# One core, attention and a feed-forward layer in one kernel: the first batch's feed-forward reordered from interleaved halves to all of the first product and then the second

## The chip, the cores and the metric

The kernel runs on one core of one Trainium2 chip. The metric is the device time of one execution in microseconds. Below, PE is the matmul engine (TensorE), PEld its weight load, DVE is VectorE, ACT is ScalarE, POOL is GpSimd, and SP issues every DMA of this kernel from one queue, in program order. Each engine works off its own queue in order.

## The reference, cut to what matters

```python
batch, n_heads, seq, head_dim = (4, 8, 768, 64)          # attention
block, window = (32, 16)
k_sum = k.reshape(B, H, nb, block, D).max(axis=3)
v_sum = v.reshape(B, H, nb, block, D).mean(axis=3)
mask_l = np.abs(pos[:, None] - pos[None, :]) < window
scores_s = scale * np.einsum('bhsd,bhnd->bhsn', q, k_sum) + np.log(block)
scores_all = np.concatenate([np.where(mask_l, scores_l, -1e9), scores_s], axis=-1)
...
x = attn_out.transpose(0, 2, 1, 3).reshape(B, S, H * D)  # (4, 768, 512)
h = x.transpose(0, 2, 1) @ U @ V                          # U (768, 32), V (32, 768)
u = x + h.transpose(0, 2, 1)
ch = np.maximum(u @ w_ch1, 0.0) @ w_ch2                   # 512 -> 2048 -> 512
return (u + ch).astype(np.float32)
```

Every query sees 31 keys around it and 24 block summaries (largest key, mean value of 32 positions). `U`, `V`, `w_ch1` and `w_ch2` are float64.

## The kernel before, in words

The four batches go through the same stages: attention by heads, the low-rank mix that gives `u`, the first product with `w_ch1` (the up product, `NF` = 16 tiles of hidden channels), ReLU, the second product with `w_ch2` (the down product), and the sum with `u`. While PE works on one batch's up and down products, the attention of the next batch is spread over that time in small steps; heads are numbered `h` = 0 to 7. All engine queues are written out by hand: an instruction stands where the Python program emits it.

Matmuls in full precision are made of three in a faster format: a matrix is split in a high part (an ACT cast) and a low part (a subtraction on DVE or POOL), and high·high, high·low and low·high are added up. A weight tile arrives as float64 words (512 KB), ACT scales the upper words (L148), DVE puts the two words together in two operations (L160, L161) into a buffer of the tag `val`, ACT casts the high part (L176) and DVE or POOL subtracts for the low part (L177, `split`). The float32 weights and sums of them (`sum_weights`) also go to DRAM for the later batches.

The opening (the word list `START`) does batch 0's attention. Then comes batch 0's own loop: for every `f` of 16 and both halves `hf` of the tokens, `up` runs 12 matmuls of 384 columns for tile `f` (L1066), `up_out` applies the ReLU and splits, and `down_rows` runs 9 matmuls of 512 columns (L1088) for the half before. The outputs of batch 0 come out with tokens in rows and are turned back by 24 PE transposes (`finish_rows`, L1109) in the up phase of batch 1. The weights of `w_ch1` and `w_ch2` arrive side by side, each through a ring of five places. In the same loop the attention of batch 1 runs by steps of its own (`one_bank_steps`), with `scores` (L348: six score tiles a head, zero-padded queries, full array).

Batches 1 and 2 have another form: `up_phase` computes the up product with seven instead of eight block products (L1352) and copies the results to SBUF; then `down_phase` runs with channels in rows: for each `f`, 12 matmuls of 512 columns and 12 of 256 columns (L1450), after `gate_high` (ACT) and `gate_low` (DVE) have made the ReLU and its low part of 768 columns. The attention of batches 2 and 3 runs in the steps of `later_step`, with `scores_by_subtiles` (L371: 24 small matmuls a head). Batch 3 uses seven products in both phases. The splits of stored weights for these batches are made by `prepare` (ACT L1016, POOL or DVE L1012).

`add_vsum` sums 32 values a block for the summaries on POOL (L258 to L272); `drip` hands out one such operation at a time. `operands` makes the operands of the next batch's seven products from `u`: for batch 1 it calls `mix_u` (three PE transposes, L733, and one matmul, L741), for later batches `add_rows`.

Of the kernel before, what the change touches and what calls it, by code (L numbers as in the profile page):

```python
# [36 lines left out]
RING = 5  # L37
# [58 lines left out]
def body(ctx: ExitStack, tc, q0, q1, k, v, vn, uv, w1, w2, mask, ident, rep, out):  # L96
# [36 lines left out]
    qd0 = [t[:, j * NH : (j + 1) * NH] for j in range(3)] + [weight_place(1, 2)[:, :NH]]  # L133
# [102 lines left out]
    def load_vsum(st, g, i):  # L236
# [4 lines left out]
        if st.b == 1 or st.b == 2 and g == 0:  # L241
            spare = hidden_place(2 + i)
# [96 lines left out]
    def scores(st, h, a):  # L339
        if h not in st.neg:  # L340
            st.neg[h] = small.tile([P, NU], F32, name="neg", bufs=4)
        qt, kt = st.qt[h].rearrange("p u q -> p (u q)"), st.kt[h]
        ps = bank("ps_s")
        for i in range(3):
            u = 3 * a + i
            j = ORDER.index(u)
            k0 = (j // 2) * KP + (j % 2) * KC
            nc.tensor.matmul(  # L348
                ps[:, i * KC : (i + 1) * KC],
                qt[:, 64 + j * P : 64 + j * P + P],  # L350
                kt[:, k0 : k0 + KC],
                start=True,
                stop=True,
            )
# [1443 lines left out]
```

## Time and profile before

| | us |
|---|---|
| runs shown | 630.95, 627.56, 630.90; median 630.9 |
| the profiled execution, whole | 628.56 |
| its span, first to last instruction | 626.8 |
| opening, to the first matmul of batch 0's up product | 50.5 |
| batch 0's loop | 50.5 to 211.3 |
| batch 1's up and down phases | 211.3 to 278.2, 278.2 to 369 |
| PE busy | 608.7 |
| PEld, DVE, ACT, POOL busy | 554.9, 417.0, 364.4, 298.6 |

The profiled execution is 2.3 us below the median of the runs; they spread over 3.4 us. PE is the bound: it is busy for 97% of the span, at a mean granted clock of 0.997, and most of what it is not busy lies in the opening. A busy PE is not PE at its peak, since matmuls overlap: the time of a stage is read from the starts of successive instructions, not from their lengths.

### The profile page before, as it was taken

How to read it: one execution, taken by the hardware profiler on the slowest of the kernel's cores; microseconds unless marked ns; L12 is line 12 of the kernel's file. 1: busy time of each engine (PE TensorE's matmuls, PEld its weight loads, DVE VectorE, ACT ScalarE, POOL GpSimd, SP SyncE). 2: the span in 40 equal slices, each digit the busy share in tenths (PEclk: the TensorE clock that was granted, in tenths of full speed). 3: DMA queues.
4: the chain of work that ended last, by engine and by line, in shares of the span. 5: the costliest groups of instructions: out<-in, count | busy, mean ns of one | idle time of the engine just before them, and what ended most of it. 6: DMA issues, size and time to landing. Idle time of an engine off the chain costs nothing.

```text
span 626.8 us, 14616 instructions
## 1 busy us (share of the span) xinstructions
PE 608.7 (97%) x5384; PEld 554.9 (89%) x5384; DVE 417.0 (67%) x1141; ACT 364.4 (58%) x828; POOL 298.6 (48%) x361
## 2 busy tenths in 40 slices
PE   4989999999999999999999999999999999999997
PEld 3779988889888999998888889998888899999997
DVE  4868867665678696477548964566546754449992
ACT  4856666656555657665444456674644456669550
POOL 2621635523246875787556966774222256630000
PEclk9989999999999999999999999999999999999999
DMA  8898499997879169888995577889997563375551
GB/s 225 230 386 269 138 314 295 289 325 256 274 204 312 53 219 298 236 260 257 271 285 175 179 258 233 250 260 274 287 280 223 160 226 120 117 223 174 159 193 51
DMA packets 94215, 144.76 MB, mean 231 GB/s; under 512 B 8896, under 2 KB 64576, under 8 KB 94144
## 3 DMA queue, kind: packets, MB, share of 16 engines
q1 hardware_dynamic: 94144, 143.82, 74.5%
q8 instruction: 43, 0.70, 0.5%
q14 instruction: 28, 0.23, 0.1%
HBM read 102.89 MB, written 40.89 MB: 229 GB/s over the span
## 4 chain that ended last, share of the span: by engine, by line
PE 90%; DMA 3%; DVE 2%; SPq 2%; issue 1%; ACT 1%; POOL 1%; ACTq 0%; POOLq 0%
PE ps_h L1352 26%; PE acc L1450 22%; PE ps_h L1066 10%; PE acc L1088 10%; PE acc L1562 9%; PE ps_x L504 3%; PE ps_s L371 2%; PE ps_s L348 2%; SPq L212 1%; DMA place<-in_v 1%; PE ps_m L699 1%; PE ps_u L733 1%; DMA whole<-up 1%; DMA place<-in_k 1%; DVE val L161 1%
## 5 line engine op out<-in xcount | busy, mean ns | idle before, releaser
L1012 POOL TENSOR_TENSOR parts<-whole,parts 128x512 fp32r<-128x512 f32 (+1 forms) x128 | 159.0, 1250 | 135.6 <-ACT parts L1016 121.0
L1352 PE MATMUL ps_h<-op,parts 128*128 128x384 f32 x1008 | 181.9, 337 | 1.0 <-ACT place L1398 0.9
L1352 PEld LDWEIGHTS ps_h<-op,parts 128*128 128x128 f32 x1008 | 174.2, 188 | 3.7 <-ACT place L1398 1.2
L1450 PE MATMUL acc<-gh,parts 128*128 128x256 f32 (+1 forms) x512 | 135.3, 342 | 0.0
L1450 PEld LDWEIGHTS acc<-gh,parts 128*128 128x128 f32 x512 | 88.3, 189 | 12.9 <-issue 1.7
L1016 ACT CAST parts<-whole 128x512 fp32r<-128x512 f32 (+1 forms) x144 | 83.5, 585 | 10.5 <-DMA whole<-sums 4.3
L1450 PE MATMUL acc<-gl,parts 128*128 128x512 f32 (+1 forms) x256 | 86.6, 338 | 0.0
L177 POOL TENSOR_TENSOR place<-val,place 128x512 fp32r<-128x512 f32 x29 | 38.5, 1348 | 87.5 <-ACT place L176 74.5
L406 ACT ACTIVATE e<-e,neg 128x120 f32<-128x120 f32 x144 | 46.5, 386 | 54.0 <-DVE neg L396 53.9
L1066 PE MATMUL ps_h<-place 128*128 128x384 f32 x384 | 73.5, 340 | 0.0
L1066 PEld LDWEIGHTS ps_h<-place 128*128 128x128 f32 x384 | 67.0, 188 | 1.8 <-DVE val L161 0.2
L1088 PE MATMUL acc<-place,gh 128*128 128x512 f32 x192 | 66.4, 401 | 0.0
L1450 PEld LDWEIGHTS acc<-gl,parts 128*128 128x128 f32 x256 | 48.6, 190 | 3.9
L1425 DVE SCALAR_TENSOR_TENSOR gl<-place,gh 128x768 fp32r<-128x768 f32 x32 | 33.8, 1056 | 20.7 <-ACT gh L1421 20.6
L396 DVE CUSTOM_DVE_ANT_0 e<-ps_s,mask_sb 128x120 f32<-128x120 f32 x144 | 32.7, 277 | 17.7 <-PE ps_s L371 9.7
L1562 PE MATMUL acc<-place,parts 128*128 128x384 f32 x246 | 43.6, 334 | 0.0
L1562 PEld LDWEIGHTS acc<-place,parts 128*128 128x128 f32 x246 | 42.7, 188 | 0.0
L1088 PEld LDWEIGHTS acc<-place,gh 128*128 128x128 f32 x192 | 36.1, 188 | 7.3
L1421 ACT ACTIVATE gh<-place 128x768 fp32r<-128x768 f32 x32 | 27.0, 844 | 22.1 <-PE acc L1450 22.0
L1078 ACT ACTIVATE gh<-ps_h 128x384 fp32r<-128x384 f32 x32 | 15.7, 491 | 40.5 <-PE ps_h L1066 40.4
L1079 DVE SCALAR_TENSOR_TENSOR gl<-ps_h,gh 128x384 fp32r<-128x384 f32 x32 | 17.8, 555 | 30.5 <-ACT gh L1078 30.5
L1088 PE MATMUL acc<-place,gl 128*128 128x512 f32 x96 | 37.7, 393 | 0.0
(166 smaller groups left out, 960.1 us busy)
## 6 DMA issues: line engine op xcount, KB each, us to landing
place<-in_w SPq DMA_DIRECT2D x32, 512.0 KB, 6.8
whole<-up SPq DMA_DIRECT2D x24, 512.0 KB, 4.3
there<-squares SPq DMA_DIRECT2D x24, 384.0 KB, 5.0
at<-there SPq DMA_DIRECT2D x96, 96.0 KB, 4.2
whole<-up SPq DMA_DIRECT2D x24, 384.0 KB, 3.6
whole<-down SPq DMA_DIRECT2D x16, 512.0 KB, 4.9
vt<-in_v SPq DMA_DIRECT2D x48, 146.2 KB, 4.3
kt<-in_k SPq DMA_DIRECT2D x24, 288.0 KB, 5.7
```

The lines of the kernel that those rows point to most:

```text
L177: engine.tensor_tensor(lo, val, f32(hi), ALU.subtract)
L396: nc.vector.tensor_tensor_reduce(out=e[:, u, :], in0=ps[:, i * KC : (i + 1) * KC], in1=mask_sb[:, m, :], scale=-SCALE, scalar=BIG, op0=ALU ...
L406: nc.scalar.activation(e[:, u, :], e[:, u, :], AF.Exp, bias=st.neg[h][:, u : u + 1], scale=-1.0,)
L1012: engine.tensor_tensor(lo, whole, f32(hi), ALU.subtract)
L1016: nc.scalar.copy(hi, whole)
L1066: nc.tensor.matmul(ps[:, :NH], w_split[0, f][:, c % 2, part_w, c // 2], ut[:, c, :], start=(n == 0), stop=(n == 3 * NC - 1),)
L1088: nc.tensor.matmul(acc[t], gt[:, sl], w_split[1, f][:, part_w], start=(first and j == 0), stop=(last and j == 2),)
L1352: nc.tensor.matmul(ps, a[:, sa, i], b[:, sb, i], start=(first and n == 0), stop=(n == 5), skip_group_check=not first,)
L1421: nc.scalar.activation(gh, h, AF.Relu)
L1425: nc.vector.scalar_tensor_tensor(gl, h, 0.0, f32(gh), ALU.max, ALU.subtract)
L1450: nc.tensor.matmul(place, w[:, part_w, c * P : (c + 1) * P], gt[:, q0:q1], start=(f == 0 and i == 0 and j == 0), stop=(f == NF - 1 and j = ...
L1562: nc.tensor.matmul(ps, w[:, part_w, off : off + P], g[part_g], start=((name, i) not in begun and j == 0), stop=(p == NF // 2 - 1 and j == ...
```

## The change: what it does

Batch 0's up product is now done for all 16 tiles first. Each result is copied to SBUF by ACT (`hidden_place`), in the form that `down_phase` expects, and then `down_phase` does batch 0's down product with channels in rows, as for batches 1 and 2. Up comes in quarters: for every tile, two token halves with two halves of the 12 matmuls each. `u` of batch 0 is put together again as `x` by POOL (`keep_rows`, eight operations of 384 columns), since `down_phase` adds `x` at the end. `finish_rows`, `leave_rows`, `up_out`, `down_rows`, `scores` and `one_bank_steps` are gone.

The 32 weight tiles go one after the other, `w_ch1` first, through one ring of eight places; step `s` of `first_weights` loads tile `s+7`, scales `s+3`, puts together `s+2` and splits `s+1`. All low parts are made by POOL now; before, the first three were made by DVE. Batch 1's attention runs in `later_step`, with `scores_by_subtiles`; thirteen of its 32 steps lie in the up phase and the others in the down phase; its spreading of key maxima goes from ACT to POOL. For batch 1, `operands` still calls `mix_u` first, and the call with `k == 4`, which is now made for batch 1 too, does as well. In the opening seven weight tiles are loaded instead of ten, the two parts of `V`'s spreading (`Q`) stand together, the mix of the first channels stands earlier, and the first up tile for both token halves is inside the opening (`U`).

```diff
-RING = 5
+RING = 8
 START = """
...
-    T13 Q1 E15 N0 M1 Mo1 C11 N3 Bp5 I0 Bd6 T8 la1 Dd5 lr Z0 Io0 C10 Dp4 T15 lb0 Y0.0 T9 Y0.1 Bp4 Dp7
...
-    N7 Jo0 I2 Qo0 lb2 Io2 Y1.0 G0.0 Qo1 J2 G1.0 Y1.1 lb4 G0.1 G1.1 Go0.0 Jo2 G0.2 G0.3 W0 Go0.1
-    Go1.1 G1.3 Go0.2 Go0.3 Go1.3 G1.2 Go1.0 Go1.2 W1 lb3 U0.0 la2 Z2
+    T13 Q1 Q0 E15 N0 Qo1 Qo0 M1 Mo1 C11 N3 Bp5 I0 Bd6 T8 lw2 Dd5 Z0 Io0 C10 Dp4 T15 lw3 Y0.0 T9
...
+    V8 V12 C15 N4 V13 V15 V14 N6 G1.0 lw5 N7 Go0.0 Go0.1 I2 Io2 U0.0.0 G1.1 Go1.0 Go1.1 lw6 J2 Jo2
+    U0.1.0 G0.2 G0.3 Go0.2 Go0.3 G1.2 G1.3 Go1.2 Go1.3 U0.0.1 U0.1.1 W1 Z2
...
+        by = nc.gpsimd.tensor_copy if st.b == 1 else nc.scalar.copy if h == 0 else nc.vector.tensor_copy
+        spread_maxima(st, h, by)
...
-            split(hi, lo, val, nc.vector if k < 2 else nc.gpsimd)
+        split(hi, lo, val, nc.gpsimd)
...
+    def up(st, hf, f, half):
+
         uh, ul = st.u[hf]
+        if half == 0:
+            begun_up[hf, f] = bank("ps_h")
+        ps = begun_up[hf, f]
+        for c in (2 * half, 2 * half + 1):
+            for j, (part_w, ut) in enumerate(((0, uh), (0, ul), (1, uh))):
                 nc.tensor.matmul(
                     ps[:, :NH],
+                    w_split[f][:, c % 2, part_w, c // 2],
                     ut[:, c, :],
...
+        if half == 1:
+            p, k = divmod(f, 2)
+            if p not in st.h:
+                st.h[p] = hidden_place(p).rearrange("p (f q) -> p f q", f=2)
+            nc.scalar.copy(st.h[p][:, k, hf * NH : (hf + 1) * NH], begun_up.pop((hf, f))[:, :NH])
+
+    def keep_rows(st, hf, c):
+
         uh, ul = st.u[hf]
+        nc.gpsimd.tensor_tensor(
+            channel_rows(st, c)[:, 3 * hf : 3 * hf + 3],
+            *(f32(t)[:, c].rearrange("p (u q) -> p u q", q=P) for t in (uh, ul)),
+            ALU.add,
+        )
+
+    def first_up_phase(st, done):
+
+        for f, hf, half in itertools.product(range(NF), range(2), range(2)):
+            if (hf, f, half) not in done:
+                up(st, hf, f, half)
+            yield
...
+    def first_weights(s, q, n):
+
+
+        f = s % NF
+
+        def turn():
+            if s + 2 < 2 * NF:
+                if s + 2 not in turning:
+                    turning[s + 2] = turn_weight(s + 2)
+                run(turning[s + 2], 1 if q == 1 else None)
+
+        if q == 0:
+            if s + RING - 1 < 2 * NF:
+                load_weight(s + RING - 1)
+            if 0 < s and s + 1 < 2 * NF:
+                split_weight(s + 1)
+            if s < NF and f % 2 == 0:
+                sum_weights(f // 2, 0)
...
+        if q == 3 and s + 3 < 2 * NF:
+            scale_weight(s + 3)
...
+    UP0 = 4 * NF - 2
+    later_start(sts[1], -6)
+    later_start(sts[1], -5)
+    for b in range(B):
...
+        steps = spread(mine, 4 if b else 8, up_last)
+        if b == 0:
+            phase = first_up_phase(cur, done)
+            for n, j in enumerate((-4, -3, -2, -1)):
+                steps.setdefault(n + 1, []).append((later_start, ahead, j))
+            for n, (hf, c) in enumerate(itertools.product(range(2), range(NC))):
+                steps.setdefault(2 * n + 3, []).append((keep_rows, cur, hf, c))
...
             do(steps.get(i, ()))
-            do(ends.get(i, ()))
+            if b == 0:
+                first_weights(i // 4, i % 4, 4)
             tick()
             drip()
...
         for i, _ in enumerate(down_phase(cur, g)):
             do(steps.get(i, ()))
+            if b == 0:
+                first_weights(NF + i // NU, i % NU, NU)
```

PE, after the opening. Before, each `f` has 12 up matmuls and 9 down matmuls for a half, in turn; the fence is the first of them in batch 0.

```order
L1066 MATMUL ps_h<-place 128x384 x24
L1088 MATMUL acc_1010<-place,gh 128x512
L1088 MATMUL acc_1010<-place,gl 128x512
L1088 MATMUL acc_1010<-place,gh 128x512
L1088 MATMUL acc_1011<-place,gh 128x512
L1088 MATMUL acc_1011<-place,gl 128x512
L1088 MATMUL acc_1011<-place,gh 128x512
L1088 MATMUL acc_1012<-place,gh 128x512
L1088 MATMUL acc_1012<-place,gl 128x512
L1088 MATMUL acc_1012<-place,gh 128x512
```

Now, at the same place (L970 is `up`, L351 the scores of batch 1, L484 its attention values):

```order
L970 MATMUL ps_h<-place 128x384 x42
L351 MATMUL ps_s<-kt,qz_84 64x120 x12
L970 MATMUL ps_h<-place 128x384 x72
L351 MATMUL ps_s<-kt,qz_85 64x120 x12
L970 MATMUL ps_h<-place 128x384 x72
L351 MATMUL ps_s<-kt,qz_84 64x120 x12
L970 MATMUL ps_h<-place 128x384 x78
L484 MATMUL ps_x<-vt,at 32x65 x24
```

The down matmuls have left; a weight tile of `w_ch1` now lasts 24 matmuls (one `f`), and of the first 42 the first 12 belong to tile 0, the rest to tiles 1 and 2.

ACT, at the end of the opening, in the kernel now: `place_954` is the place of weight tile 1, `place_1012` of tile 2, `ps_h_880` and `ps_h_904` are the up results of tile 0 for the two token halves.

```order
L682 CAST place_892<-ps_u_930 128x384
L981 COPY place_945<-ps_h_880 128x384
L981 COPY place_945<-ps_h_904 128x384
L176 CAST place_954<-val_800 128x2x256
L148 ACTIVATE place_725<-place_725 128x512
L148 ACTIVATE place_737<-place_737 128x512
L176 CAST place_1012<-val_980 128x2x256
```

The cast of tile 1 stands behind the copies of both up results of tile 0; before, the casts of this tile (L176) stood ahead of the first ReLU.

POOL, from the low part of weight tile 2 to that of tile 3, in the kernel now (L177 low part, L255 to L266 block sums of values for batch 1, L986 `keep_rows`):

```order
L177 TENSOR_TENSOR place<-val,place 128x2x256
L255 TENSOR_TENSOR place<-place 128x256
L986 TENSOR_TENSOR x<-place 128x3x128
L255 TENSOR_TENSOR place<-place 128x128
L264 TENSOR_TENSOR place<-place 128x64
L986 TENSOR_TENSOR x<-place 128x3x128
L266 TENSOR_TENSOR vsum<-vsum,place 128x64
L372 MEMSET e 128x8
L177 TENSOR_TENSOR place<-val,place 128x2x256
```

Before, POOL's first low parts in batch 0 stood two together, for one `f`, with block sums alone between them:

```order
L177 TENSOR_TENSOR place<-val,place 128x512
L177 TENSOR_TENSOR place<-val,place 128x2x256
L258 TENSOR_TENSOR place<-place 128x256
L258 TENSOR_TENSOR place<-place 128x128
L263 MEMSET vsum 128x1
L264 TENSOR_TENSOR vsum<-place 128x64
L258 TENSOR_TENSOR place<-place 128x256
L258 TENSOR_TENSOR place<-place 128x128
L267 TENSOR_TENSOR place<-place 128x64
L269 TENSOR_TENSOR vsum<-vsum,place 128x64
L258 TENSOR_TENSOR place<-place 128x256
L177 TENSOR_TENSOR place<-val,place 128x512
```

The eight `keep_rows` have come in between, two to a weight tile, and the spreading of key maxima (L328, four copies) for every head.

More of the change, by code (lines that the diff above doesn't have):

```diff
@@ L337, in value_summaries @@
         )
[L339 to L354, printed above, removed]
-        st.ps_s[h, a] = ps
     def scores_by_subtiles(st, h):
@@ L1082, in down_rows @@
-    def down_rows(acc, f, g, first, last):
-        gh, gl = g
-        for t in range(NH // P):
-            sl = slice(t * P, (t + 1) * P)
-            for j, (part_w, gt) in enumerate(((0, gh), (0, gl), (1, gh))):
-                nc.tensor.matmul(
-                    acc[t],
-                    gt[:, sl],
-                    w_split[1, f][:, part_w],
-                    start=(first and j == 0),
-                    stop=(last and j == 2),
-                )
-    def leave_rows(acc):
-        rows = []
-        for t, ps in enumerate(acc):
-            r = mo.tile([P, DM], F32, name="r", tag="val", bufs=VALS)
-            (nc.scalar.copy if t == 1 else nc.vector.tensor_copy)(r, ps)
-            rows.append(r)
-        return rows
@@ L1105, in finish_rows @@
-    def finish_rows(st, hf, rows, c):
-        ps = bank("ps_o")
-        for t, r in enumerate(rows):
-            nc.tensor.transpose(ps[:, t * P : (t + 1) * P], r[:, c * P : (c + 1) * P], ident_sb)
-        o = mo.tile([P, DM], F32, name="o", tag="val", bufs=VALS)[:, :NH]
-        uh, ul = st.u[hf]
-        nc.vector.tensor_tensor(o, ps[:, :NH], f32(uh)[:, c], ALU.add)
-        nc.vector.tensor_tensor(o, o, f32(ul)[:, c], ALU.add)
-        nc.sync.dma_start(out=out[c, :, hf * NH : (hf + 1) * NH], in_=o)
+                    start=(c == 0 and j == 0),
@@ L1224, in body @@
         "Go": lambda hf, c: mix_u_out(st, hf, c),
-        "Z": scale_weights,
-        "Y": lambda k, j: run(turns[k], len(tiles(k)) if j < 1 else None),
-        "W": split_weights,
-        "U": lambda f, hf: first.append(up_out(up(st, hf, f))),
+        "Z": scale_weight,
+        "Y": lambda m, j: run(turns[m], 1 if j < 1 else None),
+        "W": split_weight,
+        "U": lambda f, hf, half: (up(st, hf, f, half), done.add((hf, f, half))),
     }
-    first = []
+    done = set()
     for word in START.split():
@@ L1463, in down_phase @@
             yield
[L1464 removed]
+            if seen[f] == 3 and st.b:
                 prepare()
@@ L1670, in body @@
             except StopIteration as end:
-                last = end.value
+                last = end.value or []
                 break
             do(steps.get(i, ()))
-            do(ends.get(i, ()))
+            if b == 0:
+                first_weights(i // 4, i % 4, 4)
             tick()
             drip()
-            if i == UP - 8 and ahead:
+            if i == up_last - 8 and ahead:
                 g = gate_high(cur, 0)
-            if i == UP - 6 and ahead:
+            if i == up_last - 6 and ahead:
                 gate_low(*g)
```

321 lines of the change are left out of this document (76 added, 245 removed).

## The prediction

> **What bounds the kernel now.** I read the page's span, engine shares and chain first.
>
> ```profile
> span 626.8 us, 14616 instructions
> PE 608.7 (97%) x5384; PEld 554.9 (89%) x5384; DVE 417.0 (67%) x1141; ACT 364.4 (58%) x828; POOL 298.6 (48%) x361
> PE 90%; DMA 3%; DVE 2%; SPq 2%; issue 1%; ACT 1%; POOL 1%; ACTq 0%; POOLq 0%
> ```
>
> PE carries the chain, so what the change does to PE's own work shows in full, and so does every wait that it puts in front of PE. The table by stretches gives PE's slack where the change works: opening, and the two halves of batch 0's loop (columns: stretch and length, busy us of PE, PEld, DVE, ACT, POOL, then granted clock, DMA share, GB/s).
>
> ```profile
> 0.00:50.50 50.50, 38.09 (x741) 31.39 (x742) 34.20 (x172) 31.11 (x86) 17.19 (x46) 0.97 0.95 280
> 50.50:130.00 79.50, 79.50 (x563) 72.28 (x562) 58.55 (x177) 49.07 (x121) 35.10 (x48) 1.00 0.85 267
> 130.00:211.30 81.30, 80.54 (x677) 70.68 (x676) 55.28 (x125) 47.34 (x106) 36.18 (x32) 1.00 0.79 244
> ```
>
> In batch 0's loop PE lacks 0.8 us in 161: there is no waiting to be won there. Only the opening has it, 12.4 us. What can be won is PE's own work; what can be lost is the cover that the other engines have. That cover is large in the loop before: a weight pair lasts 24 up and 18 down matmuls, and POOL is busy for 44%.
>
> **The change part by part: PE's work.** The starts of successive instructions give the prices (start, length, engine, line, operation, tiles, count).
>
> ```profile
> 50.46 4.35 PE L1066 MATMUL ps_h<-place 128*128 128x384 f32 x24
> 54.65 0.39 PE L1088 MATMUL acc<-place,gh 128*128 128x512 f32 x1
> ...
> 60.91 2.27 PE L1066 MATMUL ps_h<-place 128*128 128x384 f32 x12
> 63.02 0.82 PE L348 MATMUL ps_s<-kt,qz 128*128 128x120 f32 x6
> 63.60 0.47 PE L1088 MATMUL acc<-place,gh 128*128 128x512 f32 x1
> 63.92 0.39 PE L1088 MATMUL acc<-place,gl 128*128 128x512 f32 x1
> ...
> 214.69 2.35 PE L1352 MATMUL ps_h<-op,parts 128*128 128x384 f32 x12
> 216.97 0.85 PE L371 MATMUL ps_s<-kt,qz 64*64 64x120 f32 x24
> 217.74 0.55 PE L1109 MATMUL ps_o<-ident_sb,r 128*128 128x128 f32 x3
> 218.05 2.35 PE L1352 MATMUL ps_h<-op,parts 128*128 128x384 f32 x12
> ```
>
> An up matmul takes 2.11/12 = 0.176 us (60.91 to 63.02), one weight tile of the up phase 24 of them, 4.2 us (50.46 to 54.65).
>
> Scores of batch 1. The old form takes 0.58 us to the next down matmul, which then lasts 0.32 instead of 0.23: 0.67, twice a head, 1.34. The new form: 12 up matmuls from 214.69 end at 216.80, the next instruction after the scores starts at 217.74: 0.95 a head. Eight heads win 3.1 us; I take -3.0.
>
> The transposes of `finish_rows` go: 217.74 to 218.05 is 0.31, eight times, -2.5.
>
> Down by channels has the same columns in more matmuls, 12 of 512 and 12 of 256 for 18 of 512 a tile:
>
> ```profile
> 282.10 0.62 PE L1450 MATMUL acc<-gh,parts 128*128 128x512 f32 x2
> 282.56 0.39 PE L1450 MATMUL acc<-gl,parts 128*128 128x512 f32 x1
> ...
> 284.07 0.28 PE L1450 MATMUL acc<-gh,parts 128*128 128x256 f32 x1
> ...
> 285.37 0.52 PE L1450 MATMUL acc<-gh,parts 128*128 128x256 f32 x2
> ```
>
> Two of 512 take 0.46; from 284.07 to 285.37 eleven of 256 start, 0.118 each. So 12 x 0.118 + 12 x 0.23 = 4.18 stands against 18 x 0.23 = 4.14, 16 times: +0.7.
>
> `operands` with `k == 4` calls `mix_u` for nothing, twice:
>
> ```profile
> 201.47 0.49 PE L733 MATMUL ps_u<-ident_sb,x 128*128 128x128 f32 x3
> ...
> 201.98 0.39 PE L1088 MATMUL acc<-place,gh 128*128 128x512 f32 x1
> ```
>
> 0.51 each, +1.0. The attention values, the mix and the other `mix_u` stay as they are.
>
> Opening: PE waits at the block means for their load, and the second part of `V`'s spreading now stands ahead of that wait instead of behind it.
>
> ```profile
> 34.59 1.19 PE L289 MATMUL ps_n<-place,means_w 120*32 120x65 f32 x68 [1.25 <-issue]
> 43.77 0.86 PE L1167 MATMUL ps_v<-place,ident_sb 128*32 128x192 f32 x16
> ```
>
> About 0.7 us of it falls into the wait: -0.7. Whether the new order of the rest helps cannot be read; it has the same instructions, and I bound it by 1 us either way. Tile 0 of the up product, both halves, is then done at about 54.65 - 0.7 = 54.0; I call this T.
>
> PE's work together: -3.0 - 2.5 + 0.7 + 1.0 - 0.7 = -4.5 us.
>
> **The cover that is lost.** In the up phase a weight tile lasts 4.2 us and not 8.4. The first low parts must now come from POOL, and POOL has the block sums, `keep_rows` and the key spreading in between. Its prices (mean ns of one before the second bar):
>
> ```profile
> L177 POOL TENSOR_TENSOR place<-val,place 128x512 fp32r<-128x512 f32 x29 | 38.5, 1348 | 87.5 <-ACT place L176 74.5 <-issue 6.9 <-DMA at<-there 3.4
> L258 POOL TENSOR_TENSOR place<-place 128x256 f32<-128x256 f32 x12 | 10.5, 875 | 0.1
> L258 POOL TENSOR_TENSOR place<-place 128x128 f32<-128x128 f32 x12 | 5.9, 495 | 0.5
> L794 POOL TENSOR_TENSOR op<-tmp,op 128x384 fp32r<-128x384 f32 x8 | 8.7, 1099 | 7.9 <-ACT op L790 6.3 <-DMA down<-val 1.6
> L269 POOL TENSOR_TENSOR vsum<-vsum,place 128x64 f32<-128x64 f32 x9 | 3.8, 425 | 0.5
> L267 POOL TENSOR_TENSOR place<-place 128x64 f32<-128x64 f32 x9 | 3.1, 342 | 0.6
> ```
> ```profile
> 20.61 1.18 POOL L330 COPY place<-km 64x48 f32<-64x48 f32 x4 [3.70 <-DVE km L313]
> 60.16 2.72 POOL L177 TENSOR_TENSOR place<-val,place 128x512 fp32r<-128x512 f32 x2 [20.01 <-ACT place L176]
> ```
>
> The last row says that POOL had been idle for 20 us before batch 0's first low parts: nothing held it. Now, with `keep_rows` at the 1.10 of the 384-column row, a small one at 0.34, and 0.06 between two operations (four copies of 0.246 take 1.18), the distance from one low part to the next on POOL is, by the program's order:
>
> - tile 1 to 2: 0.88 + 0.50 + 1.10 + 0.1 + 0.34 + 1.18 + 1.35 and gaps, 5.7;
> - 2 to 3: 0.88 + 1.10 + 0.50 + 0.34 + 1.10 + 0.43 + 0.1 + 1.35 and gaps, 6.2;
> - 3 to 4: the same with the four copies for the memset, 7.2;
> - 4 to 5: without either, 6.1; 5 to 6 only 3.2, since the sums have run out.
>
> From tile 1 to 5 POOL needs 25.2 us; PE wants four tiles and one head's scores, 4 x 4.2 + 0.95 = 17.8. So PE waits here, 7.4 us in all, unless the row of low parts starts early. It starts late. Tile 1's cast stands on ACT behind both copies of tile 0's results:
>
> ```profile
> L1411 ACT COPY place<-ps_h 128x384 f32<-128x384 f32 x24 | 11.4, 475 | 17.5 <-PE ps_h L1352 17.5
> L176 ACT CAST place<-val 128x512 fp32r<-128x512 f32 x32 | 18.3, 619 | 1.5 <-DVE val L161 1.3
> ```
>
> PE's last matmul of tile 0 ends some 0.25 us after T (it lasts 0.35 and is followed after 0.18); the copy is done at T + 0.8, the cast at T + 1.45, the low part at T + 2.85. PE needs the high part first and the low part at its third matmul, 0.35 us later: it waits 2.5 us. Tiles 1 to 5 then cost 2.5 + 7.4 = 9.9 us. Bounds: 4 us if POOL's operations come at the fastest that the page shows for their shapes and the block sums slip behind; 18 us with the slowest.
>
> After that ACT has one late place: the cast of tile 7 stands behind the exponentials and two value copies of head 1, estimated at +1.0 (bounds 0 and 3). The page's block sums of 256 columns took 0.74 in the early rows of batch 0 rather than 0.88, which gives 0.4 back. Waits together: +10.5. In the down phase the tile lasts 4.2 us and the attention in it, POOL has 1.35 of it, and I cost it at nothing; what hides it is POOL's free time, and without that it is up to 1 us.
>
> Sum: 628.56 (the profiled execution's whole time) - 4.5 + 10.5 = 634.6 us. That start lies 2.3 us below the median of the runs and 1 us above the fastest.
>
> One rule speaks against the change too. Rows:
>
> ```profile
> 32.50:36.00 3.50, 1.72 (x89) 1.56 (x93) 0.91 (x4) 0.12 (x2) 0.00 (x0) 0.99 1.01 390
> 36.00:39.30 3.30, 3.30 (x31) 2.86 (x23) 2.34 (x4) 2.45 (x7) 2.82 (x5) 0.50 1.04 407
> ```
>
> After a stretch in which PE was half idle, the clock was 0.50 for 3.3 us and PE lost half of that, 1.65 us. The Trainium skill (TensorE: Matmul & The Clock Gate, Part 1: The HAM clock gate) says that a window of about 3.4 us with little work halves the clock until a busy window has passed; the trace agrees in size and length. While POOL's row is the bound, a slow PE waits less for it, so I put the sum without a dip and take it as a rival.
>
> **The rivals.**
>
> (a) POOL does not hold PE: the low parts get ahead, because ACT and POOL reach tile 1 earlier or the block sums come later. For it: POOL is busy for 44% in the old loop. Against it: the order is fixed, and the distances above are sums of means. It decides if the distance falls under 4.2 to 5 us. Then 628.56 - 4.5 = 624.1.
>
> (b) POOL is slower than its means, and the kernel is slower than before: DVE gets the up product's sums and puts a tile together in 4.2 us, and POOL's operations stretch beside it. The same shape has two prices in the trace:
>
> ```profile
> L1041 POOL TENSOR_TENSOR place<-whole 128x256 f32<-128x256 f32 x8 | 8.0, 1005 | 0.0
> L1043 POOL TENSOR_TENSOR place<-whole,place 128x256 f32<-128x256 f32 x8 | 6.2, 773 | 0.0
> ```
>
> 30% more on 25.2 us is 7.6: 642.2. It decides from about 10% on, 2.5 us, where the kernel is over 1% above the median. The Trainium skill (SBUF — State Buffer, Who interferes with whom) has DVE and POOL share a port pair that one holds for a whole instruction; no row here shows a single such wait.
>
> (c) Half clock after the waits: one or two dips that outlast the waits, 1.65 us each: 636.3 to 637.9.
>
> (d) DMA. Per weight tile the up phase now stores about a quarter more, and its start still has loads for two heads: 0.85 of the DMA engines' time at 267 GB/s would become over 1. If it reaches 1.08, the phase of 74 us is stretched by 6 us: 640.6 when it adds to the waits; but the waits themselves give DMA 10 us, and the ring runs four tiles ahead.
>
> **How the numbers follow.** Chances: the forecast 0.50, (a) 0.18, (b) 0.13, (c) 0.12, (d) 0.07. The forecast alone reaches from 630 to 638.5. The range takes in most of (a), all of (c) and (d) and most of (b): 625 to 641. About 1% is what a measurement can tell, 6.3 us around 630.9: below 624.6 lies a good half of (a), 0.12; above 637.2 lie (b), most of (d), a third of (c) and the forecast's end, 0.28; between them 0.60.
>
> **What would show it.** In the changed kernel's trace: PE idle ahead of L970 with POOL as releaser (L177), near 54 to 82 us, five waits of about 2.5, 1.6, 1, 3 and 2 us, 9 to 11 in all, and hardly any after it; low parts on POOL 5.7 to 7.2 us apart there; scores of batch 1 at 0.95 us a head; PE's waits in the old trace's places unchanged after batch 1's start. Idle under 3 us there proves (a), `keep_rows` or the low part well above 1.1 and 1.35 us proves (b), a clock of 0.5 behind the waits (c), PE idle released by DMA in the up phase (d). The forecast falls if the first waits are short, or if waits of the same size appear in the later up phase or the down phase, which I cost at 1 us.

## The result, and the profile after

| | kernel before | changed kernel |
|---|---|---|
| median of the runs | 630.62 us (627.56 to 630.95, 4 runs) | 636.53 us (633.91 to 638.54, 4 runs) |
| profiled execution, its span | 628.56 us, 626.8 us | 633.91 us, 632.1 us |
| ratio after to before | | 1.0102, 95% interval 1.0053 to 1.0151 |

The change costs 5.9 us by the medians and 5.35 by the profiled executions; the forecast was +6.0 on the profiled one and 634.6 us. Measured once more beside the kernel before, the changed kernel took 637.66 us against 628.88, ratio 1.0151 (1.0111 to 1.0190), which is 8.8 us. So the change costs about 1% or a little more, and the forecast is on the low side.

The page of the changed kernel, its span, engine shares and chain:

```profile
span 632.1 us, 14968 instructions
PE 606.3 (96%) x5560; PEld 551.8 (87%) x5560; DVE 415.9 (66%) x1102; ACT 366.3 (58%) x810; POOL 324.8 (51%) x408
PE 80%; POOL 5%; issue 4%; DMA 4%; DVE 2%; ACT 2%; SPq 1%; POOLq 0%; ACTq 0%; DVEq 0%
```

PE is busy for 2.4 us less than before and yet 5.3 us later: the work went down, the waits went up. The table by stretches (length, then busy us of PE, PEld, DVE, ACT and POOL, granted clock, DMA share, GB/s) says where: opening, batch 0's up phase, batch 0's down phase.

```profile
0.00:50.50 50.50, 38.20 (x746) 31.50 (x747) 32.86 (x168) 29.51 (x85) 16.53 (x43) 1.00 0.90 255
50.50:133.00 82.50, 75.80 (x596) 70.78 (x595) 58.65 (x151) 45.30 (x100) 56.86 (x87) 0.98 0.85 262
133.00:219.97 86.97, 84.61 (x839) 71.33 (x837) 64.05 (x129) 55.15 (x110) 43.08 (x48) 1.00 0.78 238
```

In the kernel before PE lacked 0.8 us between the opening and batch 1; here it lacks 6.7 in the up phase and 2.4 in the down phase, and POOL is busy for 69% of the up phase. The waits of PE by what ended them (sum, times, longest):

```profile
PE ps_h L970 <- POOL place L177: 4.8, 4, 2.3
PE ps_h L970 <- ACT place L176: 1.9, 2, 1.1
PE ps_x L484 <- DMA at<-there: 1.3, 1, 1.3
```

L970 are the up products, L177 POOL's low parts, L176 ACT's casts, L484 the attention values. PE in order of time (start, length, line, operation, count; in brackets the idle time before it), from the end of tile 0 at 53.4 us on; the rows with a wait are at tiles 1, 2 and 4 (one of 0.47 at tile 7 follows at 91.0):

```profile
51.31 2.27 PE L970 MATMUL ps_h<-place 128*128 128x384 f32 x12
54.67 0.62 PE L970 MATMUL ps_h<-place 128*128 128x384 f32 x2 [1.09 <-ACT place L176]
56.03 4.43 PE L970 MATMUL ps_h<-place 128*128 128x384 f32 x24 [0.74 <-POOL place L177]
61.82 0.96 PE L970 MATMUL ps_h<-place 128*128 128x384 f32 x4 [1.36 <-POOL place L177]
62.72 0.85 PE L351 MATMUL ps_s<-kt,qz 64*64 64x120 f32 x24
63.49 7.77 PE L970 MATMUL ps_h<-place 128*128 128x384 f32 x42
72.05 0.62 PE L970 MATMUL ps_h<-place 128*128 128x384 f32 x2 [0.79 <-ACT place L176]
74.92 6.98 PE L970 MATMUL ps_h<-place 128*128 128x384 f32 x28 [2.25 <-POOL place L177]
81.83 0.85 PE L351 MATMUL ps_s<-kt,qz 64*64 64x120 f32 x24
```

Behind the longest wait, 28 matmuls take 6.9 us (74.92 to 81.83) where 28 x 0.176 is 4.9. The granted clock says why; it falls to 0.57 on average in the second of these stretches (a stretch at 0.50 is called half clock from here on):

```profile
71.50:75.00 3.50, 0.70 (x3) 0.38 (x3) 3.36 (x5) 2.31 (x5) 3.29 (x7) 1.00 0.91 249
75.00:79.00 4.00, 4.00 (x14) 4.00 (x15) 3.49 (x5) 0.48 (x1) 3.92 (x5) 0.57 0.62 234
79.00:81.80 2.80, 2.80 (x15) 2.26 (x14) 0.00 (x0) 1.05 (x2) 2.64 (x5) 1.00 0.07 12
```

The starts of the stages, read from PE's rows in order of time (us):

| | before | after | difference |
|---|---|---|---|
| tile 0 of the up product done | 54.65 | 53.4 | -1.2 |
| batch 1, up | 211.29 | 219.97 | +8.7 |
| batch 1, down | 278.21 | 283.88 | +5.7 |
| batch 2, down | 425.27 | 430.34 | +5.1 |
| last group of PE | 619.92 | 625.00 | +5.1 |

Everything is lost between tile 0 and batch 1's start; 3.0 us come back in batch 1's up phase, where the transposes were, and 0.6 behind it.

### The profile page after: what moved, and what is told of

Same layout as the page of the kernel before. It is cut to its first block, busy times and chain, and to the rows that moved or that the text cites. A ratio compares the mean times of both kernels' runs of the same rounds, so it can differ in the third digit from the quotient of the medians.

```text
span 632.1 us, 14968 instructions
## 1 busy us (share of the span) xinstructions
PE 606.3 (96%) x5560; PEld 551.8 (87%) x5560; DVE 415.9 (66%) x1102; ACT 366.3 (58%) x810; POOL 324.8 (51%) x408
## 4 chain that ended last, share of the span: by engine, by line
PE 80%; POOL 5%; issue 4%; DMA 4%; DVE 2%; ACT 2%; SPq 1%; POOLq 0%; ACTq 0%; DVEq 0%
PE acc L1256 27%; PE ps_h L1158 27%; PE acc L1368 9%; PE ps_h L970 8%; PE ps_s L351 3%; PE ps_x L484 3%; POOL place L177 2%; POOL place L255 1%; DMA place<-in_vn 1%; DMA at<-there 1%; DMA place<-in_q 1%; DMA whole<-up 1%; POOL x L986 1%; PE ps_m L615 1%; PE ps_t L454 1%
## 5 line engine op out<-in xcount | busy, mean ns | idle before, releaser
L912 POOL TENSOR_TENSOR parts<-whole,parts 128x512 fp32r<-128x512 f32 (+1 forms) x128 | 157.3, 1237 | 131.1 <-ACT parts L916 110.9
L177 POOL TENSOR_TENSOR place<-val,place 128x512 fp32r<-128x512 f32 x32 | 45.2, 1413 | 72.5 <-ACT place L176 49.6
L970 PE MATMUL ps_h<-place 128*128 128x384 f32 x384 | 73.0, 346 | 6.7 <-POOL place L177 4.8
L970 PEld LDWEIGHTS ps_h<-place 128*128 128x128 f32 x384 | 67.5, 192 | 10.9 <-POOL place L177 6.8
L1231 DVE SCALAR_TENSOR_TENSOR gl<-place,gh 128x768 fp32r<-128x768 f32 x48 | 50.2, 1046 | 35.2 <-ACT gh L1227 35.1
L1256 PE MATMUL acc<-gh,place 128*128 128x512 f32 (+1 forms) x256 | 67.2, 342 | 0.4 <-POOL e L372 0.2
L1227 ACT ACTIVATE gh<-place 128x768 fp32r<-128x768 f32 x48 | 40.5, 844 | 26.7 <-PE acc L1256 26.6
L1256 PEld LDWEIGHTS acc<-gh,place 128*128 128x128 f32 x256 | 44.2, 190 | 7.2 <-issue 0.9
L1256 PE MATMUL acc<-gl,place 128*128 128x512 f32 (+1 forms) x128 | 43.4, 339 | 0.2 <-DVE gl L1231 0.2
L1218 DVE TENSOR_TENSOR place<-place,ps_h 128x384 f32<-128x384 f32 x24 | 13.3, 555 | 36.1 <-ACT place L1217 36.0
L1184 DVE TENSOR_TENSOR place<-place,ps_h 128x384 f32<-128x384 f32 x24 | 13.2, 551 | 30.0 <-PE ps_h L1158 30.0
```

The source lines that it names most:

```text
L177: engine.tensor_tensor(lo, val, f32(hi), ALU.subtract)
L912: engine.tensor_tensor(lo, whole, f32(hi), ALU.subtract)
L970: nc.tensor.matmul(ps[:, :NH], w_split[f][:, c % 2, part_w, c // 2], ut[:, c, :], start=(c == 0 and j == 0), stop=(c == NC - 1 and j == 2),)
L1227: nc.scalar.activation(gh, h, AF.Relu)
L1231: nc.vector.scalar_tensor_tensor(gl, h, 0.0, f32(gh), ALU.max, ALU.subtract)
L1256: nc.tensor.matmul(place, w[:, part_w, c * P : (c + 1) * P], gt[:, q0:q1], start=(f == 0 and i == 0 and j == 0), stop=(f == NF - 1 and j = ...
```

## Experiments

The theory P: POOL's row of operations, with tile 1's late cast ahead of it, holds PE in the first up tiles. The rival R: POOL is only the last comer, and something else sets the pace. Three more came up on the way: C, a long wait of PE brings a stretch at half clock; S, POOL and DVE slow each other down, so that both are one bound; and D, a late transfer in the down phase.

The runs come in three sets, each with the kernel before beside them (medians 627.89, 628.88 and 628.89 us), and the ratios below are to that one. Only the second set holds the changed kernel; runs of the others are set against its two ratios, 1.0102 and 1.0151, so their distance from it is a range. The expectations start from its 636.5 us; what is compared is what they gain or lose against it.

### More and less on POOL's row

`keep_rows` twice in its place, and `keep_rows` later:

```diff
-steps.setdefault(2 * n + 3, []).append((keep_rows, cur, hf, c))
+steps.setdefault(2 * n + 3, []).extend([(keep_rows, cur, hf, c)] * 2)
```
```diff
-steps.setdefault(2 * n + 3, []).append((keep_rows, cur, hf, c))
+steps.setdefault(2 * n + 21, []).append((keep_rows, cur, hf, c))
```

> Edit: each of the eight keep_rows is issued twice in its place, POOL gets 8 x 1.1 us more in quarters 3 to 17; the output is the same. Theory P: the distances of low parts 1 to 5 grow by 1.16, 2.3, 2.3, 2.3 and PE waits for nearly all of it: +8.1 us, or +6 if the half-clock stretch falls inside a wait: 642.5 to 644.6. Rival R: POOL isn't what holds PE, at most 1 us more. Rival C (waits bring half clock): more waits bring more dips, each 1.7 to 2 us on top, 646 or more.

Measured: 643.92 us, ratio 1.0244 (1.0199 to 1.0289), some 6 to 9 us above the changed kernel, where P gave 6 to 8.1 and C 9.5 or more. POOL's low parts of tiles 1 to 5 in this run, in order of time:

```profile
55.13 1.29 POOL L177 TENSOR_TENSOR place<-val,place 128x512 fp32r<-128x512 f32 x1 [12.63 <-ACT place L176]
62.03 1.26 POOL L177 TENSOR_TENSOR place<-val,place 128x512 fp32r<-128x512 f32 x1
69.85 1.67 POOL L177 TENSOR_TENSOR place<-val,place 128x512 fp32r<-128x512 f32 x1
80.27 1.26 POOL L177 TENSOR_TENSOR place<-val,place 128x512 fp32r<-128x512 f32 x1
87.35 1.27 POOL L177 TENSOR_TENSOR place<-val,place 128x512 fp32r<-128x512 f32 x1
```

The distances are 6.9, 7.8, 10.4 and 7.1: 32.2 in all, where the changed kernel has 24.9, so 7.3 more for the seven added operations between them, 1.04 each. PE follows:

```profile
63.34 0.96 PE L970 MATMUL ps_h<-place 128*128 128x384 f32 x4 [2.43 <-POOL place L177]
...
71.58 6.03 PE L970 MATMUL ps_h<-place 128*128 128x384 f32 x24 [2.80 <-POOL place L177]
81.58 6.02 PE L970 MATMUL ps_h<-place 128*128 128x384 f32 x24 [3.97 <-POOL place L177]
```

Its waits at the up products grow from 6.7 to 12.6 us. P holds and R falls. In both rows of 24 that take 6.0 us in place of 4.2 the clock is at 0.50 for 3.4 us, behind the two longest waits; a third such stretch follows a wait of 1.95 us in the down phase. So C's stretches came on top of P's waits; the times alone don't part the two.

> Edit: the eight keep_rows on POOL move from quarters 3 to 17 to quarters 21 to 35 of the up phase. Theory P: the distances between low parts 1 to 5 shrink by 1.16 us for each of the seven keep_rows between them, from 5.8, 5.2, 7.8, 6.1 to about 4.6, 2.9, 5.5, 3.8; PE's waits at tile 2 (1.36 to 0.4) and tile 4 (3.0 to about 0) go, tile 1's 2.3 stays. Without those waits the half-clock stretch (75.3 to 78.9, 2.0 us) has no cause: 636.5 - 4.0 - 2.0 = 630.5 us, level with the kernel before; if the dip comes anyway, 632.5. Rival R (POOL is only the last comer): 636.5.

Measured: 633.65 us, ratio 1.0086 (1.0052 to 1.0119). The right direction and no half clock in the up phase, but less than P gave: 1 to 4 us less than the changed kernel, where 4 to 6 were forecast. The waits at tiles 2 and 4 went from 1.4 and 3.0 to 0.35 and 1.2. Later tiles wait longer, tile 7 for 0.91 in place of 0.47, and tile 11 for 0.65 in place of nothing:

```profile
72.22 5.13 PE L970 MATMUL ps_h<-place 128*128 128x384 f32 x28 [1.21 <-POOL place L177]
...
86.90 5.15 PE L970 MATMUL ps_h<-place 128*128 128x384 f32 x28 [0.91 <-POOL place L177]
```

From tile 0's end to batch 1's start this kernel needs 163.0 us and the changed kernel 166.5 (217.01 - 54.0; 219.97 - 53.4), 3.5 less. The rest of the profile gave 1.5 of that back at a wait of 1.83 us in batch 2's up phase (0.3 in the changed kernel's profile, 0.90 in the kernel before), a place that neither the change nor this edit touches and that ran from 0 to 1.95 in the profiles.

### The cast of tile 1 ahead

```diff
-... Go1.2 Go1.3 U0.0.1 U0.1.1 W1 Z2
+... Go1.2 Go1.3 W1 U0.0.1 U0.1.1 Z2
```

> Edit: the cast of weight tile 1 (W1) stands ahead of the two copies of tile 0's results instead of behind them. Theory P (tile 1's late cast and POOL's row of operations hold PE in the first up tiles): the cast starts on ACT at about 52.0 us instead of 54.0, its low part on POOL at 52.6 instead of 54.7, and the row of low parts behind it keeps its distances; PE's wait for tile 1 (1.09 + 0.74 with the cast and low part as releasers) goes, and since the row is the bound up to tile 4, the whole kernel gains the 2.1 us by which it starts earlier: 634.4 us, +3.8 over the kernel before. Rival R (something else paces the phase, such as DMA or the clock, and the releaser's name only marks the last comer): the wait for tile 1 goes but reappears further on, no change, 636.5, +5.9. If the wait at tile 2 grows by as much as tile 1's shrinks, P's row is right but its start isn't set by the cast.

Measured: 638.80 us, ratio 1.0160 (1.0120 to 1.0199): nothing was won. Tile 1's waits fell from 1.8 to 0.2 us in all, and tile 2's rose from 1.4 to 2.5 (0.20 for the cast and 2.33 for the low part):

```profile
55.22 4.11 PE L970 MATMUL ps_h<-place 128*128 128x384 f32 x22 [0.20 <-POOL place L177]
...
62.48 1.65 PE L970 MATMUL ps_h<-place 128*128 128x384 f32 x4 [2.33 <-POOL place L177]
```

The four matmuls of the last row take 1.6 us in place of 0.9: in this run half clock lasts from 61.8 to 68.7, at a cost of some 2.8 us, and it comes again behind a wait of 2.62 at tile 4. So the time is 0.6 to 3.6 us above the changed kernel, where P gave 2.1 less and R no change.

Why POOL's row moved up by only 0.4 us at tile 2, and not by 2.1 as at tile 1 (both counted from the end of tile 0), stands in DVE's rows, of the changed kernel and then of this one, for the same three sums of tiles 0 and 1 and the bit operation between them:

```profile
52.95 0.42 DVE L822 TENSOR_TENSOR place<-place,val 128x256 f32<-128x256 f32 x1
53.29 0.42 DVE L160 TENSOR_SCALAR val<-place 128x512 int32<-128x512 int32 x1
53.62 0.42 DVE L824 TENSOR_TENSOR place<-val 128x256 f32<-128x256 f32 x1
53.96 0.42 DVE L825 TENSOR_TENSOR place<-val,place 128x256 f32<-128x256 f32 x1
```
```profile
54.05 1.40 DVE L822 TENSOR_TENSOR place<-place,val 128x256 f32<-128x256 f32 x1
55.37 0.96 DVE L160 TENSOR_SCALAR val<-place 128x512 int32<-128x512 int32 x1
56.26 0.68 DVE L824 TENSOR_TENSOR place<-val 128x256 f32<-128x256 f32 x1
56.86 1.23 DVE L825 TENSOR_TENSOR place<-val,place 128x256 f32<-128x256 f32 x1
```

and in POOL's, of this kernel:

```profile
53.69 1.47 POOL L177 TENSOR_TENSOR place<-val,place 128x512 fp32r<-128x512 f32 x1 [10.93 <-ACT place L176]
...
59.41 1.67 POOL L328 COPY kt<-km 64x48 f32<-64x48 f32 x4 [1.14 <-DVE km L311]
61.16 1.26 POOL L177 TENSOR_TENSOR place<-val,place 128x512 fp32r<-128x512 f32 x1
```

In the changed kernel POOL is idle until 54.70, and DVE takes 1.4 us for these four. With POOL's low part from 53.69 on, and the block sums behind it, DVE takes 4.0. Tile 2's value and batch 1's key maxima stand behind them on DVE; POOL's key copies wait 1.14 us for these, and tile 2's low part stands behind the copies. What ACT gave, DVE took. This is the first sign of S: what delays the two engines is that they work side by side.

### Both, and the low parts on DVE

> Edit: both of the first two, the cast of tile 1 ahead of the copies and keep_rows from quarter 21 on. Theory P: no wait of the first five tiles above 0.5 us is left and no half-clock stretch: 636.5 - 8.2 = 628.3 us, 2.3 under the kernel before. If only the waits go and the dip stays: 630.3. Rival R: the time that is lost by batch 1's start (8.7 us behind the kernel before) stays in the phase in another form, over 633.

Measured: 632.56 us, ratio 1.0068 (1.0042 to 1.0094). That is 2 to 5 us less than the changed kernel, where P forecast 8.2. PE waits 1.99 us at tile 2, for the reason just seen (POOL's key copies wait 1.47 us for the key maxima there), and 1.2, 0.9 and 0.6 later.

The other way to relieve POOL is to give its low parts to DVE:

```diff
-split(hi, lo, val, nc.gpsimd)
+split(hi, lo, val, nc.vector if 2 <= m < 6 else nc.gpsimd)
```

> Edit: the low parts of weight tiles 2 to 5 are made by DVE instead of POOL, the rest of POOL's row stays. Theory P (POOL's row holds PE): no wait with POOL's low part as releaser is left at tiles 2 to 5; tile 1's 1.8 stays; DVE gets 4 x 0.7 us more, which it has free; 5 to 6 us less than the changed kernel on the same chip. Theory S (POOL and DVE slow each other while both work in SBUF, so that the row and the weight chain on DVE are one bound): DVE's part of a tile (0.42 us an operation alone, 0.5 to 1.4 beside POOL) becomes the bound instead, PE waits with DVE or ACT's cast behind it as releaser, and at most 3 us are won.

Measured: 634.51 us, ratio 1.0099 (1.0061 to 1.0137) against 1.0151 of the changed kernel in the same set: 3.2 us less by the medians. S allowed 3 and P asked for 5 to 6, but the intervals overlap, so the time alone doesn't decide; the profile does. DVE's low parts (count, then busy and mean ns of one), and PE at tile 4:

```profile
L177 DVE TENSOR_TENSOR place<-val,place 128x512 fp32r<-128x512 f32 x4 | 4.3, 1073 | 1.9 <-ACT place L176 1.9
```
```profile
72.27 7.18 PE L970 MATMUL ps_h<-place 128*128 128x384 f32 x30 [2.43 <-ACT place L176]
```

In the kernel before, the same operation takes 0.68 us on DVE (two of them, from 50 to 130 us); in this run it takes 1.07 on average (0.69 to 1.31). POOL no longer holds PE at tiles 2 to 5, and in its place the cast does at tile 4, behind a chain of weight steps on DVE. The half clock comes here too, behind the 2.43 us.

How much the two slow each other can be read over the whole stretch from 50 to 130 us of the changed kernel's profile. Of 32 single sums of 128x256 on DVE (L821 to L825), 16 had none of POOL's two-input operations beside them and took 0.41 to 0.46 us; 9 lay wholly beside such operations and took 0.43 to 1.40, 1.0 on average; the other 7, partly beside them, took 0.38 to 1.52.

### The changed kernel again, and the empty mix_u

> The changed kernel unaltered, so that this set has it on the same chip as the experiments. All theories: 1.005 to 1.015 times the kernel before, and PE's waits ahead of the first up tiles as in its first profile: about 1.1 + 0.7 for tile 1, 1.4 for tile 2, 3 for tile 4. Open is the stretch at half clock behind the long wait: if it comes with such a wait (theory C), it is there again, once; if it was chance, it is gone, and PE waits for POOL at tile 5 in its place, some 2 us.

Measured: 637.66 us, ratio 1.0151 (1.0111 to 1.0190). The waits are the same to 0.02 us (1.09, 0.75, 1.34, 0.80, 2.26), and the stretch at half clock came again in the same place: again 28 matmuls in 6.9 us. It isn't chance, as C had it. The profiled execution took 636.06 us, 2.15 more than the first one. Three places make that up: tile 0 done 0.2 later, the wait for `at<-there` in the down phase 2.30 instead of 1.33, and batch 2's wait 1.19 instead of 0.30.

```diff
-        if st.b == 1:
+        if st.b == 1 and k < 4:
             mix_u(st, hf, c)
```

> Edit: the two calls of mix_u at k == 4, whose result nobody uses, are left out (the prediction's +1.0). Forecast: 1.0 us less than the changed kernel on the same chip, and the stretch from batch 0's first down matmul to batch 1's first up matmul shorter by 1.0 than the 86.9 us of the changed kernel's profile. If PE's 0.51 each lies beside a wait there, nothing changes.

Measured: 635.75 us, ratio 1.0115 (1.0081 to 1.0149). The intervals overlap, so the time alone doesn't tell. In the profile the stretch from the first down matmul to batch 1's first up matmul is 85.8 us and not 86.9, with a wait of 1.20 instead of 1.33 in it: 1.0 us, as costed. But batch 1's up phase behind it takes 65.7 us and not 63.9, with a wait of 1.02 for ACT's copy (L1204) that the changed kernel hasn't there. So it isn't shown that the whole kernel keeps this 1.0 us.

### The wait in the down phase

The values of batch 1's last head wait for a fetch in the changed kernel. PE's row, and the DMA queue's rows before it (start, length of the issue, transfer, count):

```profile
185.16 0.89 PE L484 MATMUL ps_x<-vt,at 120*32 120x65 f32 x48 [1.33 <-DMA at<-there]
```
```profile
173.57 0.99 SPq L247 DMA_DIRECT2D place<-in_vn  x2
174.61 0.94 SPq L198 DMA_DIRECT2D kt<-in_k  x1
175.62 1.57 SPq L207 DMA_DIRECT2D qz<-in_q  x2
177.28 3.79 SPq L419 DMA_DIRECT2D at<-there  x4
```

Batch 2's first loads (`later_start` -6: the first three rows) go out just ahead of the fetch; the four parts of the fetch take 3.79 us to issue, and 2.40 at the head before.

```diff
-... for j in {7: (-6,), 9: (-5,), ...
+... for j in {7 + (b == 0): (-6,), 9: (-5,), ...
```

> Edit: in batch 0's down phase, the first loads for batch 2 (later_start -6: value rows, keys and queries of head 0) go out at weight tile 8 instead of 7, so behind the fetch of the last head's turned squares and not ahead of it. PE's wait for that fetch (DMA at<-there, 1.2 to 2.3 us in six profiles so far, 0.48 in the kernel before) was not in the prediction's sum. Theory D (these loads fill the DMA engines and the fetch lands late): the wait goes to 0.5 or less; with it the stretch at half clock that followed waits of 2 us and more; 1 to 3.5 us less than the changed kernel, 633 to 635.5. Rival: the fetch waits for the turned squares themselves or for weights in the queues, and the wait stays.

Measured: 636.17 us, ratio 1.0109 (1.0063 to 1.0156), which doesn't part it from the changed kernel's 1.0102 and 1.0151. The profile does. The fetch now goes ahead of the loads, and the row of values has no wait:

```profile
177.90 1.76 SPq L419 DMA_DIRECT2D at<-there  x4
...
181.69 0.97 SPq L247 DMA_DIRECT2D place<-in_vn  x2
```
```profile
185.97 0.89 PE L484 MATMUL ps_x<-vt,at 120*32 120x65 f32 x48
```

D holds for this wait. What it is worth in the whole kernel is not shown: the profiled execution lost more elsewhere, in the opening (tile 0 done some 2.3 us later than in the changed kernel's first profile) and at batch 2's wait of 1.95 us with a half clock behind it. A half clock came already behind tile 1's two waits there, and tile 2 then had none.

### The repairs together

First without the later loads: the cast of tile 1 and the scaling of tile 2 in the opening, weights ahead of the attention's steps, `keep_rows` later, no empty `mix_u` (its edit stands above):

```diff
-... Go1.0 Go1.1 lw6 ... Go1.2 Go1.3 U0.0.1 U0.1.1 W1 Z2
+... Go1.0 Go1.1 Z2 lw6 ... Go1.2 Go1.3 W1 U0.0.1 U0.1.1
...
-steps.setdefault(2 * n + 3, []).append((keep_rows, cur, hf, c))
+steps.setdefault(5 * n + 22, []).append((keep_rows, cur, hf, c))
...
-do(steps.get(i, ()))
 if b == 0:
     first_weights(i // 4, i % 4, 4)
+do(steps.get(i, ()))
```

> Edit: the cast of tile 1 ahead of the copies, the scaling of tile 2 in the opening, in batch 0's up phase each quarter's work on weights ahead of the attention's steps, keep_rows every fifth quarter from the 22nd on, and no mix_u at k == 4. With the cast and keep_rows alone, tile 2's low part still stood behind the key copies of batch 1's head 0, which wait for DVE. Theory P: the waits at tiles 1 to 5 fall under 0.5 us each, no stretch at half clock; from the changed kernel's 8.7 us behind the kernel before at batch 1's start 7 to 8 go, and 1.0 with mix_u: 628 us, 2 to 3 under the kernel before. Theory S: the attention's operations on DVE, now later, hold PE at the scores' banks or the transposes instead, and no more is won than with the two edits alone (about 633).

Measured: 630.30 us, ratio 1.0025 (1.0005 to 1.0044), 7.4 us less than the changed kernel, where P gave 8 to 9. It is 1.4 above the kernel before and not 2 to 3 below; S, which gave no more than the two edits alone, is off further. In the up phase up to 100 us PE waits 1.7 us in all and its clock stays at 1.00. The down phase still has its wait, here with half clock behind it:

```profile
183.80:187.00 3.20, 3.20 (x12) 2.62 (x11) 2.97 (x7) 1.57 (x3) 0.00 (x0) 0.54 0.70 238
```

Then with the later loads, `keep_rows` at quarters 21, 25, ... and no block sum in a tile's last quarter (the edit against the version just shown; that of the loads stands above):

```diff
-steps.setdefault(5 * n + 22, []).append((keep_rows, cur, hf, c))
+steps.setdefault(4 * n + 21, []).append((keep_rows, cur, hf, c))
...
-drip()
+if b or i % 4 < 3:
+    drip()
```

> Edit: the kernel with weights ahead (cast of tile 1 and scaling of tile 2 in the opening, weights ahead of the attention's steps, no empty mix_u), with batch 2's first loads at weight tile 8, keep_rows at the second quarter of tiles 5 to 12, and no block sum on POOL in a tile's last quarter. Theory P with D: PE's idle time behind the opening is under 3 us in all and no stretch at half clock is left before batch 1; 626 us, 2 to 4 under the kernel before. If POOL's work beside DVE stays the bound at single tiles, waits of 0.5 to 1 us remain and the gain is 0 to 1 us.

Measured: 625.79 us (624.73 to 627.93, 12 runs), ratio 0.9957 (0.9938 to 0.9976): 3.1 us or 0.4% faster than the kernel before, as forecast, and, by the ratios, 1.4 to 1.9% faster than the changed kernel. All waits of PE at an up product that are left:

```profile
PE ps_h L970 <- POOL place L177: 1.4, 4, 0.5
```

Behind the opening PE waits 3.3 us in all (under 3 were forecast), and the granted clock is 1.00 in every stretch from 50 to 510 us. This version is faster than both kernels. It changes several things at once, so the single repairs have no prices of their own.

## Why the prediction came out as it did

The forecast of 634.6 us lies 0.7 us above the profiled execution and 1.9 under the median. Its mechanism is right: PE's own work shrinks, and POOL's row with tile 1's late cast ahead of it holds PE in the first up tiles. That the number is so close is partly luck, since one cost was left out and others came out smaller. Step by step:

- **Scores of batch 1, -3.0.** Right. Four up matmuls from 61.82 end at 62.52, the next up matmul after the scores starts at 63.49: 0.97 a head, 0.95 forecast.
- **Transposes, -2.5.** Batch 1's up phase is 63.9 us instead of 66.9: -3.0.
- **Empty `mix_u`, +1.0.** Right in its stretch, by the run without it; whether the whole kernel pays it stays open.
- **Down by channels, +0.7.** Not measured by itself. A tile with no other work but one `mix_u` in it took 4.7 us (199.37 to 204.09); without the 0.51 that is 4.2, as costed.
- **Opening, -0.7.** Open. The first profile gave -1.2, but over the seven profiles of kernels with this opening unaltered tile 0 was done between 53.4 and 55.8 us, 54.1 on average, against 54.65 in the one profile of before. The average is 0.5 below it; the spread is larger than the term.
- **Tile 1, 2.5.** 1.09 + 0.74 of idle time and the rest in a slower start, 2.3.
- **POOL's row.** The forecast distances were 5.7, 6.2, 7.2 and 6.1, 25.2 in all. The low parts started at 54.70, 60.50, 65.66, 73.49 and 79.60: 5.8, 5.2, 7.8 and 6.1, 24.9 in all. The prices held on average, 1.16 for `keep_rows` and 1.35 for the low part:

```profile
L177 POOL TENSOR_TENSOR place<-val,place 128x512 fp32r<-128x512 f32 x15 | 20.2, 1349 | 29.5 <-ACT place L176 21.4 <-DMA at<-there 5.8 <-issue 2.1
L986 POOL TENSOR_TENSOR x<-place 128x384 f32<-128x384 f32 x8 | 9.3, 1161 | 0.1
```

- **The waits, +10.5.** The sum is nearly right and its parts are partly wrong. Tiles 2 and 4 came as forecast (1.4 and 3.0, against 1.6 and 3). Tile 3 had none, because `keep_rows` took 1.00 there and two block sums 0.73 and 0.45. Tile 5 had none either: behind tile 4's wait PE ran at half clock, 2.0 us longer, while POOL's low part came. So rival (c) happened, but in place of a wait, as the sum without a dip had assumed; it came again in the same place in each of the three profiles of a kernel with this row unaltered that were taken later. Tile 7 was 0.5 for 1.0. In all 6.7 us of idle time and 2.0 of half clock in the up phase. Each of the six waits costs some 0.16 more than its idle time, because a matmul lasts 0.34 us and the next one would start 0.176 after it: 9.7 in all.
- **The down phase "at nothing", up to 1 us.** This is the step that failed. PE waits 2.4 us there, 1.7 more than before, and in other executions of the same down phase up to 3.3, at times with half clock on top. The prediction's own sign for it came true: a wait of 1.33 us, as long as tile 2's, in the down phase. The cover that the prediction named was POOL's free time, but what came late was a transfer: it didn't follow that batch 2's first loads now stand on the queue right ahead of the last head's fetch. In the kernel before the same fetch goes out at 186.03, and these loads follow from 189.26 on. Whether this is also why the median lies above the profile and the forecast isn't shown: in the second profile of the changed kernel 1.0 of the 2.15 us more are this wait, but the run with the later loads isn't parted from the changed kernel by its time.

For the stretch up to batch 1's start this makes -1.2 (opening) + 6.7 + 2.0 (idle time and clock, up) - 3.0 + 0.7 + 1.0 + 1.7 (idle time, down) = 7.9 us; with 0.16 more for each of the nine waits that are new it is 9.3. Measured are 8.7, between the two, and 8.5 were forecast. So the waits of the up phase were 0.8 less than forecast, the opening 0.5 earlier in this profile, and the down phase's waits made up for both: this is the luck in the number.

**The rivals.** (a), POOL doesn't hold PE, falls by the doubled `keep_rows`. (b), POOL slower than its means by DVE, falls in the form it had: POOL's means held. But its mechanism is there, in the other direction: POOL slows DVE. The prediction said of the rule of the Trainium skill (SBUF — State Buffer, Who interferes with whom) that no row showed a single such wait. The rows of DVE above show it, 0.42 us alone and up to 1.4 beside POOL. The trace of the kernel before had such rows, too: there L923, the same sum as L822 now, took 0.42 us at 54.42, when POOL was idle, and 1.40 beside two low parts of POOL:

```profile
70.08 2.73 POOL L177 TENSOR_TENSOR place<-val,place 128x512 fp32r<-128x512 f32 x2 [2.64 <-DMA qz<-in_q]
71.69 1.40 DVE L923 TENSOR_TENSOR place<-place,val 128x256 f32<-128x256 f32 x1
```

The rule says that an instruction of DVE with two inputs in SBUF contends with one of GpSimd that reads SBUF; the sums agree, and so does the bit operation L160 (0.42 to 0.96), of a kind that the page lists as able to contend. It didn't spoil the forecast, but the reasoning on the first repair: moving POOL's work forward moved the collision, too. (d), DMA in the up phase, falls: the share is 0.99 from 97 to 133 us, and PE has no wait for DMA there.

The last version is the cross-check of the sum. Its tile 0 is done at 54.7 us, as in the kernel before, so the opening is out of the comparison. From there to batch 1's start it takes 156.9 us, the kernel before 156.6: -3.0 for scores and +0.7 for channels, and 2.8 us of idle time where before had 0.7, makes -0.2 against the measured +0.3. Then 2.3 us are won in batch 1's up phase, where the transposes were. The gain that the change has in PE's work is real; the changed kernel paid it and more for the order on POOL and on the queue.

## What to carry to other kernels

When a change halves the time that PE spends on a tile, add up, for each engine that makes the next tile, all that stands in its queue between two tiles; where the sum is above PE's time, PE waits. The distances worked out this way held here within 2% in sum (25.2 against 24.9 us), with single ones up to 1 us off. An operation moved between POOL and DVE, or forward in time on one of them, changes what the other's operations cost, so a repair has to be read in both queues. Also follow the DMA queue: a small fetch that somebody waits for must not stand right behind the next batch's large loads.

## What the hardware showed

**Half clock after a wait of 2 us.** Over the twelve profiles, behind the opening, there were 16 waits of PE of 1.95 us or more, several of them the same place in different runs. With 12 of them, within some 1.5 us of the wait's end, the granted clock went to 0.50 for 3.4 us (once 6.8), at a cost of 1.5 to 2 us (once 3). Of 30 shorter ones from 0.7 us on, one was followed so (tile 1's two in a row are counted as one, and tile 4's short wait with its long one). In the 4 us up to the end of one of the 16 PE had still been busy for 0 to 2.1 us. The Trainium skill (TensorE: Matmul & The Clock Gate, Part 1: The HAM clock gate) gives a free-running window of about 3.4 us, and an idle window as the condition for the slow clock. The length agrees, and that the same 2.3 us wait in the down phase brought half clock in one run (2.29) and none in another (2.30) fits a window that runs free. Read as a window without any work, the condition doesn't agree: of the 12 waits only one (3.97) was as long as such a window, and the measurement decides. So a wait near 2 us can cost nearly twice its length.

**POOL and DVE.** A single sum on DVE took up to three times as long and more beside POOL's two-input sums (1.40 us for 0.42), and somewhat over twice as long on average (1.0). POOL's own low part varied less, from 1.26 to 1.67 us in the rows above.
